# Loads queued further ahead in places shared with the weights, and output stores held back behind gating copies, in a fused attention and softplus kernel

## The chip, the cores and the metric

The kernel runs on one core of a Trainium2 chip. The metric is the device time of one execution in microseconds (us), the median of several runs. One execution per kernel is also profiled; its *span* is from first to last instruction. A run more than 1.5% above the fastest of its kernel counts as slow, and ratios use fast runs alone.

Engines: PE is TensorE (matmul), DVE VectorE, ACT ScalarE, POOL GpSimd, SP SyncE. DMA is the core's 16 DMA engines.

## The reference

Linear attention per head (8 batches, 8 heads, 576 positions, 64 features), then a two-layer network with a softplus.

```python
r = maximum(x, 0); phi(x) = concat([r * cos, r * sin])     # cos, sin of the position
kv  = einsum('bhsf,bhsd->bhfd', phi(k), v);  z = sum(phi(k), over s)
num = einsum('bhsf,bhfd->bhsd', phi(q), kv); den = einsum('bhsf,bhf->bhs', phi(q), z) + 1e-6
x   = (num / den), heads side by side                       # 4608 x 512
h   = x @ w_in                                              # 512 -> 2048
out = (maximum(h, 0) + log1p(exp(-abs(h)))) @ w_out         # 2048 -> 512
```

The softplus is replaced by its linear part where a bound on the norms of x and w_in allows it: `x @ (0.5 * w_in @ w_out) + ln 2 * sum(w_out)`. The kernel computes the bound while it runs, and a flag at the end chooses whether a slow exact branch must follow. With these inputs it need not.

## The kernel before

q, k and v are 3 x 8 loads of 1.18 MB in float32, converted to bf16 on the way and issued from GpSimd. The weights (8.4 MB) are loaded between batch 0 and batch 1. The output is made in 36 tiles of 128 tokens; a tile is 0.262 MB. The loads and the places they go to:

```python
loads = tile_pool(name="loads", bufs=3)                   # 3 places for each of q, k, v
kqv[b, name] = loads.tile([128, 4, T, D], BF16, tag=name)
w_out_sb = singles.tile([128, FO, D_MODEL], BF16)         # own places for the weights
w_inT    = singles.tile([128, FO, D_MODEL], BF16)
...
fetch(2)                                                  # right after batch 1's loads
```

One iteration of the main loop, for tile i (cut):

```python
attend(i)                       # PE: num, den; DVE: rden = 1/den, x = num * rden
scale_values(...)               # DVE: v * cos, v * sin of a later batch
if b + 3 < B and j == 1: fetch(b + 3)       # GpSimd: three loads
if ...: pool_relu(b + 2)        # GpSimd: rectify k, then q, of batch b + 2
if more and left < 2: key_values(b + 1, 1 - left)
turn_queries(i + 2)             # PE: q transposed and scaled; ACT: to SBUF
turn_x(i - 1)                   # PE: x transposed; ACT: to SBUF
finish(*emit(i - 2))            # PE: x @ W_c; DVE: + bias; then the store
```

The end of an iteration:

```python
def finish(n, ps):
    o_sb = outs.tile([128, D_MODEL], F32, tag="o_sb")     # 4 places
    nc.vector.tensor_add(o_sb, ps, b_bc)
    store(n, o_sb)                                        # SyncE: one DMA; two for a pair tile
```

Transposed queries of a whole batch share one tile (`qTs[b]`, three places of 9.2 KB per partition).

Of the kernel before, what the change touches and what calls it, by code (L numbers as in the profile page):

```python
# [21 lines left out]
def kernel(  # L22
# [25 lines left out]
    singles = ctx.enter_context(tc.tile_pool(name="singles", bufs=1))  # L48
    loads = ctx.enter_context(tc.tile_pool(name="loads", bufs=3))
    work = ctx.enter_context(tc.tile_pool(name="work", bufs=2))  # L50
# [17 lines left out]
    def load(b, name, part=None):  # L68
        if not part:
            kqv[b, name] = loads.tile([128, 4, T, D], BF16, tag=name, name=f"{name}_sb")  # L70
        hps = slice(0, 4) if part is None else slice(2 * part, 2 * part + 2)
        src = SRC[name][b].rearrange("(hp h2) (p t) d -> (h2 p) hp (t d)", h2=2, t=T)
        nc.gpsimd.dma_start(  # L73
            kqv[b, name].rearrange("p h t d -> p h (t d)")[:, hps], src[:, hps]
        )
# [10 lines left out]
    )  # L86
    w_out_sb = singles.tile([128, FO, D_MODEL], BF16)
    BLOCKS = 8
    FB = FO // BLOCKS
    w_in_r = moe_w_in.rearrange("(ko p) f -> p ko f", p=128)  # L90
    w_out_r = moe_w_out.rearrange("(fo p) m -> p fo m", p=128)

    warm = singles.tile([128, 2 * D_MODEL], BF16)
    nc.vector.memset(warm, 1.0)  # L94
# [11 lines left out]
    for j in range(BLOCKS):  # L106
        cols = slice(128 * FB * j, 128 * FB * (j + 1))
        nc.gpsimd.dma_start(w_in_sb[:, :, cols], w_in_r[:, :, cols])
        nc.gpsimd.dma_start(w_out_sb[:, FB * j : FB * (j + 1), :], w_out_r[:, FB * j : FB * (j + 1), :])

    w_sum = loads.tile([128, 2, D_MODEL], F32, tag="k", name="w_sum")
    w_tmp = loads.tile([128, 2, D_MODEL], F32, tag="v", name="w_tmp")
    load(1, "v")
# [58 lines left out]
    b_bc = singles.tile([128, D_MODEL], F32)  # L172
    w_inT = singles.tile([128, FO, D_MODEL], BF16)

# [18 lines left out]
    def turn_w_in(j):  # L193
        ps = o_ps.tile([128, FB, KO, 128], BF16, tag="o", name="wT_ps")
        for f in range(FB):
            for ko in range(KO):
                ft = FB * j + f
                nc.tensor.matmul(
                    ps[:, f, ko, :], w_in_sb[:, ko, ft * 128 : (ft + 1) * 128], ident,
                    is_transpose=True, start=True, stop=True, skip_group_check=True,  # L200
                )

        for f in range(FB):
            (nc.scalar.copy if f % 2 else nc.vector.tensor_copy)(
                view(w_inT, [256, 2], [64, 2], [128, 2], [1, 64], offset=(FB * j + f) * D_MODEL),
                view(ps, [256, 2], [128, 2], [64, 2], [1, 64], offset=f * D_MODEL),
            )
# [3 lines left out]
    def square_w(ft):  # L211
        if ft % 2 or ft >= 10:
            nc.scalar.activation(
                w_square[:, 0, :], w_inT[:, ft, :], ACT.Square, bias=zero_b,
                accum_out=w_norm[:, ft : ft + 1],
            )
        else:
            nc.vector.scalar_tensor_tensor(
                w_square[:, 1, :], w_inT[:, ft, :], 1.0, w_inT[:, ft, :], ALU.mult, ALU.mult,
                accum_out=w_norm[:, ft : ft + 1],  # L220
            )

    def fold(j, ps):
        order = [(ft, g) for ft in range(FB * j, FB * (j + 1)) for g in range(KO)]
        if j == BLOCKS - 1:
            order.sort(key=lambda x: x[1])
        for ft, g in order:
            nc.tensor.matmul(  # L228
                ps[g // 2][:, g % 2, :], w_inT[:, ft, g * 128 : (g + 1) * 128], w_out_sb[:, ft, :],
                start=(ft == 0), stop=(ft == FO - 1),  # L230
            )


    def sum_w_out(quarter):
        rows = w_out_sb[:, 4 * quarter : 4 * quarter + 4, :]
        nc.vector.tensor_add(w_tmp if quarter else w_sum, rows[:, :2, :], rows[:, 2:, :])
        if quarter:
            nc.vector.tensor_add(w_sum, w_sum, w_tmp)
            nc.vector.tensor_add(w_tmp[:, 0, :], w_sum[:, 0, :], w_sum[:, 1, :])

    def bias():
        ps = o_ps.tile([128, D_MODEL], F32, tag="o", name="b_ps")
        nc.tensor.matmul(ps, ones, w_tmp[:, 0, :], start=True, stop=False)
        for ft in range(8, FO):
            nc.tensor.matmul(ps, ones_b, w_out_sb[:, ft, :], start=False, stop=(ft == FO - 1))
        nc.scalar.mul(b_bc, ps, LN2)
# [60 lines left out]
    def turn_queries(n, pool=None, split=False):  # L307
        ps = (pool or qt_ps).tile([128, 2, 512], F32, tag="big" if pool else "qt", name="q_ps")
        if len(tiles[n]) == 1:
            b, t = tiles[n][0][0], tiles[n][0][1] // 64  # L310
            if b not in qTs:
                qTs[b] = work.tile([128, 2, 4, S], BF16, tag="qT", name="qT", bufs=3)
            parts = [(b, hq, t + t2) for hq in range(2) for t2 in range(2)]
            moves = [(view(qTs[b], [4 * S, 2], [64, 2], [S, 4], [1, 64], offset=64 * t), ps)]
        else:
            parts = [(p[0], hq, T - 1) for p in tiles[n] for hq in range(2)]
            moves = [
                (view(qTs[p[0]], [4 * S, 2], [S, 4], [1, 64], offset=512), ps[:, j])
                for j, p in enumerate(tiles[n])
            ]  # L320
        for j, (b, hq, t) in enumerate(parts):
# [3 lines left out]
                start=True, stop=True, skip_group_check=True,  # L325
            )
        if split:
            moves = [
                (view(qTs[b], [64, 2], [S, 4], [1, 64], offset=64 * (t - 1) + hq * 4 * S), ps[:, hq])
                for hq in range(2)  # L330
            ]
        for j, (dst, src) in enumerate(moves):
            copy = nc.vector.tensor_copy if split and j else nc.scalar.copy
            copy(dst, view(src, [1, 1024 // len(moves)]))  # L334

    xs = {}

    def attend(n, pool=None):
# [7 lines left out]
        for g in range(4):  # L346
            hq, h2 = g // 2, g % 2
            for b, t0, m, p0 in tiles[n]:
                for c in range(2):
                    for i in range(2):  # L350
                        rows = slice(64 * i, 64 * i + 64)
                        nc.tensor.matmul(  # L352
                            num[p0 : p0 + m, i, C * g : C * g + C],
                            qTs[b][rows, hq, 2 * c + h2, t0 : t0 + m],
                            blk_bufs[b % 3][rows, hq, h2, c, :], start=False, stop=(c == 1),
                            skip_group_check=True,
                        )
        rden = small.tile([128, 2, 4], F32, tag="rden")
        nc.vector.reciprocal(rden, view(num, [512, 2], [C, 4], offset=D))
        if n % 2 == 0:  # L360
            xs[n // 2] = outs.tile([128, 2, 4, 2, D], BF16, tag="x", name="x", bufs=4)
# [36 lines left out]
    def emit(n, ps=None):  # L398
# [4 lines left out]
        return n, ps  # L403

    def finish(n, ps):
        o_sb = outs.tile([128, D_MODEL], F32, tag="o_sb")
        nc.vector.tensor_add(o_sb, ps, b_bc)  # L407
        store(n, o_sb)

# [32 lines left out]
    for j in range(BLOCKS + 1):  # L442
# [22 lines left out]
        if j == 6:  # L465
            mark_values(1)
    for hq in range(2):
        for c in range(2):
# [16 lines left out]
    turn_queries(5, big_ps)  # L485
    fetch(3)
    pool_relu(2)
    LEAD = 2

# [4 lines left out]
    for b in range(1, B):  # L494
# [6 lines left out]
        for j, i in enumerate(mine):  # L501
# [5 lines left out]
            if j == len(mine) - 1 and b + 2 < B:  # L507
                scale_values(b + 2, *SCALES[0])
            if b + 3 < B and j == 1:
                fetch(b + 3)  # L510
            if b + 2 < B and j == (3 if b == 1 else 2):
                pool_relu(b + 2)
            left = mine[-1] - i
            if more and left < 2:
# [29 lines left out]
    with tc.If(flag < 1):  # L544
        one_b = small.tile([128, 1], F32, tag="one_b", bufs=1)
        nc.vector.memset(one_b, 1.0)
        w_g = [view(vcs_bufs[g // 2], [1, D_FF], offset=g % 2 * D_FF) for g in range(KO)]
        for ft in range(FO):
            ps = qt_ps.tile([128, KO, 128], BF16, tag="qt", name="w_ps")
            for g in range(KO):  # L550
                nc.tensor.matmul(
                    ps[:, g, :], w_inT[:, ft, g * 128 : (g + 1) * 128], ident,
                    is_transpose=True, start=True, stop=True, skip_group_check=True,
                )
            for g in range(KO):
                nc.vector.tensor_copy(w_g[g][:, ft * 128 : (ft + 1) * 128], ps[:, g, :])
        for n in range(len(tiles)):
            soft = loads.tile([128, FO, 128], BF16, tag="k", name="soft")
            for quarter in range(4):
                h = qt_ps.tile([128, 4, 128], F32, tag="qt", name="h_ps")  # L560
                for j in range(4):
                    ft = 4 * quarter + j
                    for g in range(KO):
# [3 lines left out]
                        )  # L567
                e = outs.tile([128, 4, 128], F32, tag="o_sb", name="e")
                nc.scalar.activation(e, h, ACT.Abs, bias=zero_b)
# [6 lines left out]
            for ft in range(FO):  # L576
                nc.tensor.matmul(
                    ps, soft[:, ft, :], w_out_sb[:, ft, :], start=(ft == 0), stop=(ft == FO - 1)
                )
            o_sb = outs.tile([128, D_MODEL], F32, tag="o_sb")  # L580
            nc.vector.tensor_copy(o_sb, ps)
# [31 lines left out]
```

## Time and profile before

| | before |
|---|---|
| time, median of 3 | 142.99 us (142.59 to 143.39) |
| profiled run | 145.22 us, span 143.3 (slow: over 1.5% above the fastest) |
| busy: PE, DVE, ACT, POOL | 118.8, 105.4, 94.7, 66.4 us |
| read from HBM, written | 36.70 MB, 9.44 MB |
| chain that ended last | 63% of the span is waiting for DMA |

The chain that ended last, by engine (shares of the span):

```profile
DMA 63%; POOL 10%; issue 10%; PE 7%; ACT 5%; DVE 0%; POOLq 0%
```

The chain starts at the last instruction and steps back to whatever released it each time. That nearly two thirds of it are DMA says that the end moves when loads move; it doesn't say whether they are late because they were issued late or because the engines were busy with something else. The lines in the prediction are about that.

### The profile page before, as it was taken

Reading aid. Unit: us, or ns where it says so; the run is one execution under the profiler, and the core shown is the slowest. Engines: PE = TensorE matmul, PEld = TensorE weight load, DVE = VectorE, ACT = ScalarE, POOL = GpSimd, SP = SyncE. Lnnn points to the kernel's source line nnn. Section 1 sums busy time; section 2 is a strip of 40 time slices with the busy share of each in tenths; the row PEclk is TensorE's granted clock in tenths of the full one; section 3 lists DMA queues with packets and bytes.
Section 4 is the critical chain, followed back from the end, with each engine's and each line's share of the span. In section 5 each row is a group of like instructions: output and inputs, shape, how many; then the busy total and the mean of one; then the engine's idle time right before and its main releaser. Section 6 shows DMA issues by size and latency. Waiting matters only on the chain.

```text
span 143.3 us, 4481 instructions
## 1 busy us (share of the span) xinstructions
PE 118.8 (83%) x1890; PEld 76.1 (53%) x1890; DVE 105.4 (74%) x219; ACT 94.7 (66%) x165; POOL 66.4 (46%) x83
## 2 busy tenths in 40 slices
PE   4927978999799999997899979799889729998810
PEld 1414455666345657774666746476666516665300
DVE  2499244797798589989889988779969953576920
ACT  3401194597698476898599978599969904998500
POOL 7995455564018089266856825936620570000000
PEclk9996599999999999999999999999999986999975
DMA  1999999999999999999999999999999730233350
GB/s 12 176 186 198 205 197 201 200 201 206 207 206 209 209 236 271 242 255 249 240 245 260 254 254 251 249 250 238 260 246 258 219 77 0 90 134 146 136 170 11
DMA packets 24410, 28.14 MB, mean 196 GB/s; under 512 B 1344, under 2 KB 19776, under 8 KB 24384
## 3 DMA queue, kind: packets, MB, share of 16 engines
q0 software_dynamic: 19136, 18.35, 78.2%
q1 hardware_dynamic: 5248, 9.44, 19.7%
q8 instruction: 17, 0.28, 0.7%
q14 instruction: 9, 0.07, 0.1%
HBM read 36.70 MB, written 9.44 MB: 322 GB/s over the span
## 4 chain that ended last, share of the span: by engine, by line
DMA 63%; POOL 10%; issue 10%; PE 7%; ACT 5%; DVE 0%; POOLq 0%
DMA q_sb<-in_q_dram 43%; DMA w_out_sb<-in_moe_w_out_dram 15%; DMA v_sb<-in_v_dram 5%; POOL q_r L258 4%; POOL k_sb L73 3%; PE o_ps L402 3%; ACT qT L334 2%; POOL v_sb L73 2%; ACT x L380 2%; PE q_ps L322 1%; PE o_big L402 1%; ACT xT_all L375 1%; PE xT_ps L371 1%; PE num_ps L352 1%; POOL q_sb L73 1%
## 5 line engine op out<-in xcount | busy, mean ns | idle before, releaser
L334 ACT CAST qT<-q_ps 128x1024 bf16<-128x1024 f32 (+1 forms) x40 | 35.7, 909 | 17.8 <-PE q_ps L322 17.8
L402 PE MATMUL o_ps<-W_c,xT_all 128*128 128x512 bf16 x132 | 34.8, 387 | 0.7 <-DVE o_sb L407 0.6
L407 DVE TENSOR_TENSOR o_sb<-o_ps,b_bc 128x512 f32<-128x512 f32 x33 | 22.6, 686 | 13.4 <-PE o_ps L402 13.4
L275 DVE TENSOR_TENSOR vcs<-v_sb,cs_wide 128x1152 bf16<-128x1152 bf16 x32 | 29.7, 944 | 0.0
L322 PE MATMUL q_ps<-diag,q_r 128*128 128x256 bf16 x144 | 23.3, 283 | 7.7 <-POOL q_r L258 5.9
L362 DVE TENSOR_TENSOR x<-num_ps,rden 128x512 bf16<-128x512 f32 x36 | 24.9, 692 | 2.1
L251 POOL TENSOR_SCALAR k_sb<-k_sb 128x1152 bf16<-128x1152 bf16 x12 | 14.7, 1232 | 22.8 <-DMA k_sb<-in_k_dram 22.8
L258 POOL TENSOR_SCALAR q_r<-q_sb 128x1152 bf16<-128x1152 bf16 x13 | 16.8, 1312 | 15.8 <-DMA q_sb<-in_q_dram 15.8
L375 ACT CAST xT_all<-xT_ps 128x512 bf16<-128x512 f32 x36 | 21.5, 598 | 1.2 <-PE xT_ps L371 1.2
L380 ACT ACTIVATE x<-x,zero_b 128x1024 bf16<-128x1024 bf16 x17 | 19.8, 1162 | 0.0
L322 PEld LDWEIGHTS <-q_r 128*128 128x128 bf16 x144 | 12.1, 100 | 13.5 <-POOL q_r L258 7.3
L402 PEld LDWEIGHTS <-xT_all 128*128 128x128 bf16 x144 | 12.9, 99 | 10.3 <-issue 1.6
L352 PE MATMUL num_ps<-kvblk,qT 64*128 64x65 bf16 (+1 forms) x640 | 15.8, 194 | 0.0
L228 PE MATMUL wc_ps<-w_out_sb,w_inT 128*128 128x512 bf16 x64 | 15.0, 380 | 0.0
L289 PE MATMUL kv_ps<-vcs,k_sb 64*64 64x132 bf16 x576 | 11.8, 225 | 3.7 <-DVE vcs L275 3.7
L294 ACT CAST kvblk<-kv_ps 128x260 bf16<-128x260 f32 x16 | 6.0, 376 | 11.5 <-PE kv_ps L289 11.0
L371 PE MATMUL xT_ps<-perm,x 128*128 128x128 bf16 x128 | 12.7, 222 | 0.6 <-ACT xT_all L375 0.6
L289 PEld LDWEIGHTS <-k_sb 64*64 64x64 bf16 x576 | 9.5, 110 | 5.8 <-issue 4.4
L371 PEld LDWEIGHTS <-x 128*128 128x128 bf16 x144 | 10.8, 99 | 2.2 <-issue 0.6
L352 PEld LDWEIGHTS <-qT 64*128 64x128 bf16 (+1 forms) x640 | 11.4, 98 | 0.8
L342 PEld LDWEIGHTS <-warm 128*128 128x128 bf16 x72 | 6.9, 99 | 9.1 <-issue 2.1
L414 PE MATMUL spin_ps<-warm 128*128 128x512 bf16 x28 | 9.4, 498 | 2.0 <-DVE warm L94 2.0
(75 smaller groups left out, 131.8 us busy)
## 6 DMA issues: line engine op xcount, KB each, us to landing
out_dram<-o_sb SPq DMA_DIRECT2D x32, 256.0 KB, 6.2
v_sb<-in_v_dram POOLq DMA_DIRECT2D x7, 576.0 KB, 14.5
k_sb<-in_k_dram POOLq DMA_DIRECT2D x7, 576.0 KB, 16.9
q_sb<-in_q_dram POOLq DMA_DIRECT2D x6, 576.0 KB, 20.3
xT_all<-in_moe_w_in_dram POOLq DMA_DIRECT2D x8, 256.0 KB, 10.5
w_out_sb<-in_moe_w_out_dram POOLq DMA_DIRECT2D x8, 256.0 KB, 10.6
q_sb<-in_q_dram POOLq DMA_DIRECT2D x4, 288.0 KB, 10.5
out_dram<-o_sb SPq DMA_DIRECT2D x8, 128.0 KB, 3.9
```

What stands on the lines that cost most here:

```text
L258: engine.tensor_scalar(q_rs[b][:, hq], view(kqv[b, "q"], [D, T], [T * D, 2], [1, D], offset=2 * hq * T * D), BIG, 0.0, ALU.min, ALU.max,)
L275: nc.vector.tensor_mul(view(vcs, [T * 2 * VW, 2], [2 * VW, T], [1, D], offset=2 * hq * T * 2 * VW + c * VW), kqv[b, "v"][:, 2 * hq : 2 * h ...
L289: nc.tensor.matmul(kv[64 * i : 64 * i + 64, h2, :, :VW], k_r[rows, 2 * hq + i, t, :], vcs[rows, 2 * hq + i, t, :, :], start=(t == 0), stop ...
L322: nc.tensor.matmul(ps[:, j // 2, 256 * (j % 2) : 256 * (j % 2) + 256], q_rs[b][:, hq, t, :, :], diag[:, t, :, :], start=True, stop=True, s ...
L334: copy(dst, view(src, [1, 1024 // len(moves)]))
L352: nc.tensor.matmul(num[p0 : p0 + m, i, C * g : C * g + C], qTs[b][rows, hq, 2 * c + h2, t0 : t0 + m], blk_bufs[b % 3][rows, hq, h2, c, :], ...
L362: nc.vector.tensor_mul(xs[n // 2][:, n % 2], view(num, [C, 4], [512, 2], [1, D]), view(rden, [1, 4], [4, 2], [0, D]),)
L371: nc.tensor.matmul(ps[:, g, :], x[:, g, :, :], perm if len(tiles[n]) == 1 else ident, start=True, stop=True, skip_group_check=True,)
L375: nc.scalar.copy(xT_all[:, n], ps)
L380: nc.scalar.activation(x, x, ACT.Square, bias=zero_b, accum_out=x_norm[:, n : n + 1])
L402: nc.tensor.matmul(ps, xT_all[:, n, g, :], W_c[:, g, :], start=(g == 0), stop=(g == 3))
L407: nc.vector.tensor_add(o_sb, ps, b_bc)
```

## The change

The intent: stores and loads run on the same DMA engines, and the loads are urgent while the stores are not. So up to 11 finished tiles are held in SBUF, and their stores go out when the loads are nearly done. Moreover loads get more places, which the weights use first (their tiles die early), and batch 3 is fetched before GpSimd first stops to rectify. SBUF for the held tiles comes from transposed queries kept by tile rather than by batch.

```diff
-    loads = ctx.enter_context(tc.tile_pool(name="loads", bufs=3))
+    loads = ctx.enter_context(tc.tile_pool(name="loads", bufs=6))
+            kqv[b, name] = loads.tile(... tag=name, bufs=4 if name == "q" else 6)
-    w_out_sb = singles.tile([128, FO, D_MODEL], BF16)
-    w_inT = singles.tile([128, FO, D_MODEL], BF16)
+        if j % 2 == 0:
+            w_out_tiles.append(loads.tile([128, 4, D_MODEL], BF16, tag="k", ...))
+            w_inT_tiles.append(loads.tile([128, 4, D_MODEL], BF16, tag="v", ...))
... (w_sum and w_tmp move to the places of q; fetch(3) moves up, fetch(b + 3) becomes fetch(b + 4))
-                qTs[b] = work.tile([128, 2, 4, S], BF16, tag="qT", name="qT", bufs=3)
+        qT = qTs[n] = work.tile([128, 2, 4, 128], BF16, tag="qT", name="qT", bufs=4)
...
         nc.vector.reciprocal(rden, view(num, [512, 2], [C, 4], offset=D))
+        pass_stores(n, rden)
...
+    HOLD = 11
+    held = []
+    passed = singles.tile([1, 4, 8], F32)
+    def pass_stores(i, rden):
+        keep = HOLD - 1 - 3 * max(0, i - 27)
+        if len(held) > keep:
+            nc.sync.dma_start(passed[:, i % 4, :], rden[:1].rearrange("p i g -> p (i g)"))
+        while len(held) > max(0, keep):
+            store(*held.pop(0))
     def finish(n, ps):
-        o_sb = outs.tile([128, D_MODEL], F32, tag="o_sb")
+        o_sb = outs.tile([128, D_MODEL], F32, tag="o_sb", bufs=HOLD + 3)
         nc.vector.tensor_add(o_sb, ps, b_bc)
-        store(n, o_sb)
+        held.append((n, o_sb))
+        if n > last - 3:
+            while held:
+                store(*held.pop(0))
... (the exact branch, not taken here, loads its weights again)
```

The gating copy is a DMA of 32 bytes that copies a tile's reciprocals to nowhere in particular. The stores stand behind it in SyncE's program, so while SyncE waits for the reciprocal of tile i, they wait too: in the changed kernel the first store goes out at 72.98 us, right after the first copy, and without the copies at 48.01 (e7 below).

More of the change, by code (lines that the diff above doesn't have):

```diff
@@ L69, in load @@
         if not part:
-            kqv[b, name] = loads.tile([128, 4, T, D], BF16, tag=name, name=f"{name}_sb")
+            kqv[b, name] = loads.tile(
+                [128, 4, T, D], BF16, tag=name, name=f"{name}_sb", bufs=4 if name == "q" else 6
+            )
         hps = slice(0, 4) if part is None else slice(2 * part, 2 * part + 2)
@@ L86, with w_out_rows, w_inT_rows @@
     )
-    w_out_sb = singles.tile([128, FO, D_MODEL], BF16)
     BLOCKS = 8
     FB = FO // BLOCKS
+    w_out_tiles, w_inT_tiles = [], []
+    def w_out_rows(ft, count=1):
+        return w_out_tiles[ft // 4][:, ft % 4 : ft % 4 + count, :]
+    def w_inT_rows(ft):
+        return w_inT_tiles[ft // 4][:, ft % 4, :]
     w_in_r = moe_w_in.rearrange("(ko p) f -> p ko f", p=128)
     w_out_r = moe_w_out.rearrange("(fo p) m -> p fo m", p=128)
-    warm = singles.tile([128, 2 * D_MODEL], BF16)
+    warm = singles.tile([128, D_MODEL], BF16)
     nc.vector.memset(warm, 1.0)
@@ L108 @@
         nc.gpsimd.dma_start(w_in_sb[:, :, cols], w_in_r[:, :, cols])
-        nc.gpsimd.dma_start(w_out_sb[:, FB * j : FB * (j + 1), :], w_out_r[:, FB * j : FB * (j + 1), :])
-    w_sum = loads.tile([128, 2, D_MODEL], F32, tag="k", name="w_sum")
-    w_tmp = loads.tile([128, 2, D_MODEL], F32, tag="v", name="w_tmp")
+        if j % 2 == 0:
+            w_out_tiles.append(loads.tile([128, 4, D_MODEL], BF16, tag="k", name="w_out_sb"))
+            w_inT_tiles.append(loads.tile([128, 4, D_MODEL], BF16, tag="v", name="w_inT"))
+        nc.gpsimd.dma_start(w_out_rows(FB * j, FB), w_out_r[:, FB * j : FB * (j + 1), :])
+    w_sum = loads.tile([128, 2, D_MODEL], F32, tag="q", name="w_sum", bufs=4)
+    w_tmp = loads.tile([128, 2, D_MODEL], F32, tag="q", name="w_tmp", bufs=4)
     load(1, "v")
@@ L204, in turn_w_in @@
             (nc.scalar.copy if f % 2 else nc.vector.tensor_copy)(
-                view(w_inT, [256, 2], [64, 2], [128, 2], [1, 64], offset=(FB * j + f) * D_MODEL),
+                view(w_inT_rows(FB * j + f), [256, 2], [64, 2], [128, 2], [1, 64]),
                 view(ps, [256, 2], [128, 2], [64, 2], [1, 64], offset=f * D_MODEL),
@@ L213, in square_w @@
             nc.scalar.activation(
-                w_square[:, 0, :], w_inT[:, ft, :], ACT.Square, bias=zero_b,
+                w_square[:, 0, :], w_inT_rows(ft), ACT.Square, bias=zero_b,
                 accum_out=w_norm[:, ft : ft + 1],
@@ L218, in square_w @@
             nc.vector.scalar_tensor_tensor(
-                w_square[:, 1, :], w_inT[:, ft, :], 1.0, w_inT[:, ft, :], ALU.mult, ALU.mult,
+                w_square[:, 1, :], w_inT_rows(ft), 1.0, w_inT_rows(ft), ALU.mult, ALU.mult,
                 accum_out=w_norm[:, ft : ft + 1],
@@ L228, in fold @@
             nc.tensor.matmul(
-                ps[g // 2][:, g % 2, :], w_inT[:, ft, g * 128 : (g + 1) * 128], w_out_sb[:, ft, :],
+                ps[g // 2][:, g % 2, :], w_inT_rows(ft)[:, g * 128 : (g + 1) * 128], w_out_rows(ft)[:, 0],
                 start=(ft == 0), stop=(ft == FO - 1),
@@ L234, in sum_w_out @@
     def sum_w_out(quarter):
-        rows = w_out_sb[:, 4 * quarter : 4 * quarter + 4, :]
+        rows = w_out_rows(4 * quarter, 4)
         nc.vector.tensor_add(w_tmp if quarter else w_sum, rows[:, :2, :], rows[:, 2:, :])
@@ L244, in bias @@
         for ft in range(8, FO):
-            nc.tensor.matmul(ps, ones_b, w_out_sb[:, ft, :], start=False, stop=(ft == FO - 1))
+            nc.tensor.matmul(ps, ones_b, w_out_rows(ft)[:, 0], start=False, stop=(ft == FO - 1))
         nc.scalar.mul(b_bc, ps, LN2)
@@ L308, in turn_queries @@
         ps = (pool or qt_ps).tile([128, 2, 512], F32, tag="big" if pool else "qt", name="q_ps")
+        qT = qTs[n] = work.tile([128, 2, 4, 128], BF16, tag="qT", name="qT", bufs=4)
         if len(tiles[n]) == 1:
             b, t = tiles[n][0][0], tiles[n][0][1] // 64
-            if b not in qTs:
-                qTs[b] = work.tile([128, 2, 4, S], BF16, tag="qT", name="qT", bufs=3)
             parts = [(b, hq, t + t2) for hq in range(2) for t2 in range(2)]
-            moves = [(view(qTs[b], [4 * S, 2], [64, 2], [S, 4], [1, 64], offset=64 * t), ps)]
         else:
-            parts = [(p[0], hq, T - 1) for p in tiles[n] for hq in range(2)]
-            moves = [
-                (view(qTs[p[0]], [4 * S, 2], [S, 4], [1, 64], offset=512), ps[:, j])
-                for j, p in enumerate(tiles[n])
-            ]
+            parts = [(p[0], hq, T - 1) for hq in range(2) for p in tiles[n]]
         for j, (b, hq, t) in enumerate(parts):
@@ L327, in turn_queries @@
         if split:
-            moves = [
-                (view(qTs[b], [64, 2], [S, 4], [1, 64], offset=64 * (t - 1) + hq * 4 * S), ps[:, hq])
-                for hq in range(2)
-            ]
-        for j, (dst, src) in enumerate(moves):
-            copy = nc.vector.tensor_copy if split and j else nc.scalar.copy
-            copy(dst, view(src, [1, 1024 // len(moves)]))
+            for hq in range(2):
+                (nc.vector.tensor_copy if hq else nc.scalar.copy)(
+                    view(qT, [64, 2], [128, 4], [1, 64], offset=512 * hq), ps[:, hq]
+                )
+        else:
+            nc.scalar.copy(view(qT, [512, 2], [64, 2], [128, 4], [1, 64]), view(ps, [1, 1024]))
     xs = {}
@@ L353, in attend @@
                             num[p0 : p0 + m, i, C * g : C * g + C],
-                            qTs[b][rows, hq, 2 * c + h2, t0 : t0 + m],
+                            qTs[n][rows, hq, 2 * c + h2, p0 : p0 + m],
                             blk_bufs[b % 3][rows, hq, h2, c, :], start=False, stop=(c == 1),
@@ L357, in attend @@
                         )
-        rden = small.tile([128, 2, 4], F32, tag="rden")
+        rden = small.tile([128, 2, 4], F32, tag="rden", bufs=6)
         nc.vector.reciprocal(rden, view(num, [512, 2], [C, 4], offset=D))
+        pass_stores(n, rden)
         if n % 2 == 0:
@@ L466 @@
             mark_values(1)
+            fetch(3)
     for hq in range(2):
@@ L485 @@
     turn_queries(5, big_ps)
-    fetch(3)
     pool_relu(2)
+    fetch(4)
     LEAD = 2
@@ L508 @@
                 scale_values(b + 2, *SCALES[0])
-            if b + 3 < B and j == 1:
-                fetch(b + 3)
             if b + 2 < B and j == (3 if b == 1 else 2):
                 pool_relu(b + 2)
+                if b + 4 < B:
+                    fetch(b + 4)
             left = mine[-1] - i
@@ L547 @@
         w_g = [view(vcs_bufs[g // 2], [1, D_FF], offset=g % 2 * D_FF) for g in range(KO)]
-        for ft in range(FO):
-            ps = qt_ps.tile([128, KO, 128], BF16, tag="qt", name="w_ps")
-            for g in range(KO):
-                nc.tensor.matmul(
-                    ps[:, g, :], w_inT[:, ft, g * 128 : (g + 1) * 128], ident,
-                    is_transpose=True, start=True, stop=True, skip_group_check=True,
-                )
-            for g in range(KO):
-                nc.vector.tensor_copy(w_g[g][:, ft * 128 : (ft + 1) * 128], ps[:, g, :])
+        for g in range(KO):
+            for i in range(2):
+                rows = (4 * (g // 2) + 2 * i + g % 2) * D
+                nc.gpsimd.dma_start(w_g[g][64 * i : 64 * i + 64], moe_w_in[rows : rows + D, :])
+        w_out_tiles.clear()
+        for j in range(4):
+            w_out_tiles.append(loads.tile([128, 4, D_MODEL], BF16, tag="k", name="w_out_sb"))
+            nc.gpsimd.dma_start(w_out_rows(4 * j, 4), w_out_r[:, 4 * j : 4 * j + 4, :])
         for n in range(len(tiles)):
-            soft = loads.tile([128, FO, 128], BF16, tag="k", name="soft")
+            soft = loads.tile([128, FO, 128], BF16, tag="v", name="soft")
             for quarter in range(4):
@@ L567 @@
                         )
-                e = outs.tile([128, 4, 128], F32, tag="o_sb", name="e")
+                e = outs.tile([128, 4, 128], F32, tag="o_sb", name="e", bufs=HOLD + 3)
                 nc.scalar.activation(e, h, ACT.Abs, bias=zero_b)
@@ L577 @@
                 nc.tensor.matmul(
-                    ps, soft[:, ft, :], w_out_sb[:, ft, :], start=(ft == 0), stop=(ft == FO - 1)
+                    ps, soft[:, ft, :], w_out_rows(ft)[:, 0], start=(ft == 0), stop=(ft == FO - 1)
                 )
-            o_sb = outs.tile([128, D_MODEL], F32, tag="o_sb")
+            o_sb = outs.tile([128, D_MODEL], F32, tag="o_sb", bufs=HOLD + 3)
             nc.vector.tensor_copy(o_sb, ps)
```

## The prediction

> **What bounds the kernel now.** I read the page's slices first. Slices are 3.58 us wide, and the three rows that matter here are the matmul engine, the DMA engines and the bytes moved:
>
> ```profile
> PE   4927978999799999997899979799889729998810
> DMA  1999999999999999999999999999999730233350
> GB/s 12 176 186 198 205 197 201 200 201 206 207 206 209 209 236 271 242 255 249 240 245 260 254 254 251 249 250 238 260 246 258 219 77 0 90 134 146 136 170 11
> ```
>
> The DMA engines are never idle until slice 31 (111 us), then they are two thirds empty to the end. PE is also near full, except for one hole in slice 32 (115 to 118 us). Next, what the bytes are: the loads convert float32 to bf16 on the way, so a load reads twice the bytes it lands, and the queue view says who moved what.
>
> ```profile
> q0 software_dynamic: 19136, 18.35, 78.2%
> q1 hardware_dynamic: 5248, 9.44, 19.7%
> HBM read 36.70 MB, written 9.44 MB: 322 GB/s over the span
> ```
>
> Queue q0 holds the loads, q1 the stores. Before any store (20 to 30 us) the windows view gives 200 GB/s landed, so 400 GB/s read. In 75 to 85 us it gives 253 GB/s; about four stores of 0.262 MB are 105 of it, the loads then land 148 and read 296: again 401 GB/s of memory traffic. So loads and stores share one budget of about **0.40 MB/us**, and a store delays the loads by 0.262/0.40 = 0.66 us.
>
> The chain of waits that ended last says where that hurts (start, us, what):
>
> ```profile
> 93.30 21.47 DMA q_sb<-in_q_dram
> ...
> 114.92 2.77 POOL q_r L258 x2
> 117.69 0.05 issue
> 117.73 0.61 PE q_ps L322 x2
> ```
>
> The last batch's queries land at 114.77 us; GpSimd rectifies them, and only then can PE turn them. From there 25.6 us of compute and stores follow to 143.3. How regular is the rest? VectorE makes one reciprocal per tile of 128 tokens (36 tiles), so its timeline is a clock of progress (start, us):
>
> ```profile
> 49.89 0.20 DVE L359 RECIPROCAL rden<-num_ps 128x8 f32<-128x8 f32 x1
> 70.75 0.20 DVE L359 RECIPROCAL rden<-num_ps 128x8 f32<-128x8 f32 x1
> 82.39 0.20 DVE L359 RECIPROCAL rden<-num_ps 128x8 f32<-128x8 f32 x1
> 114.20 0.19 DVE L359 RECIPROCAL rden<-num_ps 128x8 f32<-128x8 f32 x1
> 121.12 0.20 DVE L359 RECIPROCAL rden<-num_ps 128x8 f32<-128x8 f32 x1
> ```
>
> These are tiles 4, 12, 17, 29 and 30. Tiles 12 to 17 take 2.33 us each; 4 to 12 take 2.61; 17 to 29 take 2.65; tile 29 to 30 alone takes 6.92. So there is a compute pace near 2.35 and, on top, waits for loads: small ones in each batch and one of about 4 us at the end. The waits of 105 to 120 us agree:
>
> ```profile
> POOL k_sb L251 <- DMA k_sb<-in_k_dram: 6.0, 1, 6.0
> PE q_ps L322 <- POOL q_r L258: 3.3, 2, 2.1
> DVE o_sb L407 <- PE o_ps L402: 1.5, 2, 1.1
> ```
>
> So the start is DMA bound (to 42.4 us, when batch 1's queries are in), then compute and DMA are nearly matched, with DMA slightly slower.
>
> **What the Trainium skill says.** "DMA: Bandwidth & Descriptors", section "Queues, rings and completion order": each DMA engine goes round-robin between its queue rows packet by packet, so stores from SyncE and loads from GpSimd slow each other. The trace agrees (0.40 MB/us with or without stores). "HBM Reference", section "Access": one core streaming alone reaches about 425 GB/s; this trace has 400 to 416. "DMA: Bandwidth & Descriptors", section "Anatomy of one DMA": some 2 us of fixed cost per DMA, mostly completion; no gating copy runs in the kernel before, but its smallest landing time, 2.3 us for a store in the quiet tail, fits. "SBUF — State Buffer", section "Who interferes with whom": a VectorE instruction with two SBUF inputs and a GpSimd one that reads SBUF block each other. In the trace the value scaling takes 0.75 us, and up to 1.73 where GpSimd rectifies; the change leaves those, so I count them in the pace.
>
> **The change part by part.**
>
> (1) Deeper load buffers, the weights in shared places, batch 3 fetched before batch 2 is rectified. This keeps two batches queued, where one and a bit was. By itself I give it **0 us**: the DMA row is at 9 throughout to 111 us, so no load was issued too late for the engines to stay busy. The order of instructions on GpSimd shows that the new early loads wait for buffers freed by the folding of the weights and for the DMA eight issues back, all done before 42.4 us, so the start doesn't get longer.
>
> (2) Stores held. Up to 11 finished tiles wait; tile n is stored after the reciprocal of tile n+13 rather than after its own bias add, which comes during iteration n+2. At most 11 x 0.262 = 2.88 MB is out of the loads' way, worth 2.88/0.40 = 7.2 us of load time. When do loads end then? At 42.4 us batches 2 to 7 remain: 6 x 3 x 1.18 = 21.2 MB. At pace 2.38 (my estimate between 2.33 and 2.42, the pace of tiles 4 to 9, 49.89 to 62.00 us), the first store comes with tile 13, at 49.9 + 9 x 2.38 = 71.3 us. Till then 28.9 x 0.40 = 11.6 MB are read; the remaining 9.7 MB share with stores of 0.262/2.38 = 0.11 MB/us, so take 9.7/0.29 = 33.4 us: **loads end near 104.7 us** in place of 114.8. At 0.385 MB/us, the slowest stretches of this trace, it is 108.
>
> (3) Is that soon enough? With no wait, tile 29's reciprocal stands at 49.9 + 25 x 2.38 = 109.4 us. The last queries are wanted there, rectified, so they should land by some 3 us earlier, 106.4. With 104.7 there is no hole; with 108 one of about 2 us. Tile 30 follows 2.75 us after tile 29 (an iteration with keys times values): 112.1 in place of 121.1, **a gain of 9.0 us**, and the tail from there is unchanged (22.2 us): 134.3.
>
> (4) Gating copies: 23 DMAs of 32 bytes in SyncE's queue. They cost no engine time; SyncE spends about 0.54 us per issue, as for a store. 23 + 40 issues x 0.54 = 34 us over 70 us: it keeps up.
>
> (5) Queries turned into a tile of their own rather than a batch's: the split copies of the four pair tiles (two of 0.53 us) become one of 1.01: 0. The smaller warm-up tile: under 0.3 us in a start that loads bound: 0.
>
> (6) A new wait. An output buffer is used again after 14 tiles, and the store of tile n-14 is issued only after the reciprocal of n-1. From there to the bias add of tile n are three iterations and 1.5 us, 8.6 us; a gating issue, a store issue and a landing of 6.2 (5.9 to 7.6 under load) take 7.3 to 8.7 us. Just covered; I charge 0.3 us. Bursts of four stores at tiles 28, 29 and 30 drain at 4 x 0.66 = 2.6 us per iteration, about one iteration each, while 30 us remain; if the last load is still coming they delay it.
>
> Sum: 143.0 - 9.0 + 0.3 = 134.3; for half a chance of a remaining hole of about 2 us I add 1.1: **135.4 us**.
>
> **The rivals.**
>
> (a) Compute is already the bound, and only the hole goes: PE, VectorE and ScalarE are each over 90% busy in 75 to 85 us. Then the pace stays 2.6 and only 6.92 - 2.75 = 4.2 us are won: 138.8. For it: the full engines. Against: every batch has a wait of PE for rectified queries, and tiles 12 to 17 ran at 2.33.
>
> (b) The new wait takes its place: VectorE waits for stores to land before each bias add from tile 14 on. If a landing takes 8 us with the gate and not 6, each loop of three tiles is 1 to 2 us longer, some 5 us in all over the 15 held tiles: 139 to 140. For it: the margin of (6) is thin. Against: landings over 7 us are rare in this trace.
>
> (c) The bursts at 28 and 29 meet the last load. Eight stores are 5.2 us of traffic; if loads run late these come on top: q at 110, end at 138. It needs loads at 108 or later.
>
> (d) The held stores become the tail. 21 tiles after tile 27 are 5.5 MB, 13.8 us at 0.40 MB/us, with 30 us left: unlikely; +1 at most.
>
> **Range and chances.** Between no hole with a pace of 2.33 (133) and rival (b) or (c) (139.5): 132.5 to 139.5. Over 2% faster means below 140.1, which even the rivals mostly give: 0.89. Within 2%: 0.09, if two of the rivals come together. Slower: 0.02.
>
> **What the changed profile would show.** GB/s near 205 until about 70 us, then 250: no stores before tile 13. The last q landing at 104 to 108 us, and in the reciprocals a step from tile 29 to 30 below 4 us. The pace from tile 4 to 29 near 2.4. VectorE's bias adds waiting for DMA under 1 us in all. A DMA row that is higher after 110 us than the present 2 to 3 tenths. I am wrong if the loads end before 106 us and the pace is still 2.6 (rival a), if the bias adds wait for stores (b), or if GB/s doesn't stay at the 0.40 budget when the stores go.

## The result, and the profile after

| | before | after |
|---|---|---|
| time, median of 4 | 143.06 us (142.59 to 143.39) | 137.16 us (136.77 to 137.93) |
| ratio of fast runs | | 0.9596, 95% interval 0.9546 to 0.9647 |
| span of the profiled run | 143.3 (slow run) | 136.1 (fast run) |
| spans of all four runs | | 136.1, 134.9, 135.5, 135.1 |

A ratio is the mean time of one kernel's fast runs over that of the other's of the same rounds, so it isn't quite the ratio of the medians. A span is 1.8 to 1.9 us shorter than the time of that same run (136.1 against 137.93, 143.3 against 145.22). The change is 4.0% faster; the predicted 135.4 us (132.5 to 139.5) was 1.8 us too low, and the range holds the result.

The slices of the changed kernel's page (now 3.40 us each):

```profile
PE   5926959999699998998969998999999999989400
DMA  1999999999999999999999999999996365776480
GB/s 8 179 184 200 201 202 199 200 202 202 207 207 207 208 207 210 207 209 207 208 209 207 228 262 256 253 251 256 241 277 208 117 205 200 288 245 234 180 289 15
```

GB/s now stays at 200 to 210 until slice 21 (71 to 75 us): nothing but loads. Then it rises to some 250, loads and stores. The DMA row falls at slice 30 (102 us) and afterwards stands mostly at 5 to 8 tenths in place of 2 to 3: the held stores. PE has no hole like the one at 115 us any more.

The chain that ended last, by engine:

```profile
PE 49%; DVE 22%; ACT 15%; issue 6%; POOL 2%; ACTq 0%; POOLq 0%; DVEq 0%
```

DMA has left the chain altogether. GpSimd's timeline (start, us of two instructions, and in brackets the idle time and what ended it) shows the last queries landing just before 105.62:

```profile
105.62 2.76 POOL L269 TENSOR_SCALAR q_r<-q_sb 128x1152 bf16<-128x1152 bf16 x2 [2.06 <-DMA q_sb<-in_q_dram]
```

VectorE's reciprocals, tiles 4, 29, 30 and 35:

```profile
47.96 0.20 DVE L364 RECIPROCAL rden<-num_ps 128x8 f32<-128x8 f32 x1
110.07 0.20 DVE L364 RECIPROCAL rden<-num_ps 128x8 f32<-128x8 f32 x1
112.53 0.20 DVE L364 RECIPROCAL rden<-num_ps 128x8 f32<-128x8 f32 x1
123.81 0.20 DVE L364 RECIPROCAL rden<-num_ps 128x8 f32<-128x8 f32 x1
```

From 29 to 30 it is now 2.46 us, not 6.92. But from tile 35 to the end of the span it is 12.3 us, where the kernel before took 10.8 (132.50 to 143.3). SyncE's own timeline explains why (start, us for the group, and how many):

```profile
119.16 1.25 SPq L402 DMA_DIRECT2D out_dram<-o_sb  x2
120.51 0.68 SPq L420 DMA_DIRECT2D passed<-rden  x1
121.23 1.22 SPq L400 DMA_DIRECT2D out_dram<-o_sb  x2
...
126.74 0.69 SPq L420 DMA_DIRECT2D passed<-rden  x1
127.84 1.85 SPq L400 DMA_DIRECT2D out_dram<-o_sb  x3
129.79 1.21 SPq L402 DMA_DIRECT2D out_dram<-o_sb  x2
```

The gating copy at 126.74 belongs to tile 35, whose reciprocal had been ready since 124.0: SyncE is nearly 3 us behind. From 108.12 to 131.0 it issues 8 copies and 24 stores, 32 issues in 22.9 us, almost without pause. The span ends 5.1 us after SyncE's last issue, and in e5 below, whose last issue comes earlier, 5.2 us after it.

### The profile page after: what moved, and what is told of

It reads as the page before. It is cut to its first block, busy times and chain, and to the rows that moved or that the text cites. A ratio compares the mean times of both kernels' runs of the same rounds, so it can differ in the third digit from the quotient of the medians.

```text
span 136.1 us, 4522 instructions
## 1 busy us (share of the span) xinstructions
PE 114.9 (84%) x1890; PEld 74.7 (55%) x1890; DVE 102.6 (75%) x219; ACT 94.5 (69%) x161; POOL 66.5 (49%) x83
## 4 chain that ended last, share of the span: by engine, by line
PE 49%; DVE 22%; ACT 15%; issue 6%; POOL 2%; ACTq 0%; POOLq 0%; DVEq 0%
PE o_ps L408 11%; PE q_ps L327 9%; DVE vcs L286 8%; ACT qT L339 8%; PE wc_ps L239 8%; PE kv_ps L300 6%; PE num_ps L357 5%; PE xT_ps L377 3%; DVE o_sb L426 3%; DVE x L368 3%; ACT xT_all L381 3%; ACT x L386 3%; DVE diag L161 2%; PE wT_ps L209 2%; PE o_big L408 1%
## 5 line engine op out<-in xcount | busy, mean ns | idle before, releaser
L339 ACT CAST qT<-q_ps 128x1024 bf16<-128x1024 f32 x34 | 34.3, 1014 | 8.2 <-PE q_ps L327 8.1
L408 PE MATMUL o_ps<-W_c,xT_all 128*128 128x512 bf16 x132 | 33.9, 379 | 0.8 <-DVE o_sb L426 0.7
L286 DVE TENSOR_TENSOR vcs<-v_sb,cs_wide 128x1152 bf16<-128x1152 bf16 x32 | 28.0, 891 | 0.6 <-DMA v_sb<-in_v_dram 0.6
L327 PE MATMUL q_ps<-diag,q_r 128*128 128x256 bf16 x144 | 21.9, 274 | 1.6 <-issue 0.5
L377 PE MATMUL xT_ps<-perm,x 128*128 128x128 bf16 x128 | 12.4, 219 | 0.6 <-ACT xT_all L381 0.6
L436 PE MATMUL spin_ps<-warm 128*128 128x512 bf16 x28 | 8.6, 468 | 1.5 <-DVE warm L104 1.5
```

The lines of the kernel that those rows point to most:

```text
L286: nc.vector.tensor_mul(view(vcs, [T * 2 * VW, 2], [2 * VW, T], [1, D], offset=2 * hq * T * 2 * VW + c * VW), kqv[b, "v"][:, 2 * hq : 2 * h ...
L327: nc.tensor.matmul(ps[:, j // 2, 256 * (j % 2) : 256 * (j % 2) + 256], q_rs[b][:, hq, t, :, :], diag[:, t, :, :], start=True, stop=True, s ...
L339: nc.scalar.copy(view(qT, [512, 2], [64, 2], [128, 4], [1, 64]), view(ps, [1, 1024]))
L377: nc.tensor.matmul(ps[:, g, :], x[:, g, :, :], perm if len(tiles[n]) == 1 else ident, start=True, stop=True, skip_group_check=True,)
L408: nc.tensor.matmul(ps, xT_all[:, n, g, :], W_c[:, g, :], start=(g == 0), stop=(g == 3))
```

## The experiments

e0 and e10 are the kernel before, e4 is the changed kernel and e5 is e3 again. All the others were timed beside the kernel before on the same chip. Medians are of all runs. For reading them together, these are positions in each profile (us of the span): when GpSimd starts to rectify the last queries, the reciprocal of tile 30, and the tail from tile 35's reciprocal to the end.

| run | stores held | last q rectified | tile 30 | tail | time, median | ratio (95%) |
|---|---|---|---|---|---|---|
| before, first profile (slow run) | 0 | 114.92 | 121.12 | 10.8 | 142.99 | |
| e0 before | 0 | 113.87 | 118.81 | 11.0 | 142.94 | |
| e10 before | 0 | 114.55 | 119.08 | 10.8 | 142.95 | |
| e1 deep loads alone (slow run) | 0 | 114.38 | 119.81 | 11.1 | 143.10 | 1.003 (0.996 to 1.009) |
| e7 no gates | 0 in effect | 113.98 | 118.50 | 10.9 | 142.26 | 1.000 (0.992 to 1.007) |
| e6 five held | 5 | 111.75 | 116.19 | 10.8 | 140.84 | 0.987 (0.976 to 0.999) |
| changed | 11 | 105.62 | 112.53 | 12.3 | 137.16 | 0.960 (0.955 to 0.965) |
| e4 changed (slow run) | 11 | 106.31 | 113.07 | 12.3 | 137.84 | 0.960 (0.954 to 0.966) |
| e2 hold alone | 11 | 106.17 | 112.17 | 12.4 | 137.52 | 0.959 (0.949 to 0.968) |
| e3 tail ungated | 11 | 106.02 | 112.77 | 10.9 | 136.75 | 0.961 (0.954 to 0.967) |
| e5 tail ungated | 11 | 105.81 | 111.31 | 10.5 | 136.40 | 0.958 (0.953 to 0.963) |
| e8 first 15 stores left out | all | 99.47 | 113.53 | 12.1 | 137.79 | 0.963 (0.958 to 0.968) |
| e11 little rectifying | 11 | | 110.97 | 11.9 | 135.68 | 0.951 (0.945 to 0.957) |

**e0 and e10: the kernel before, profiled again.** No edit.

> The kernel before, unchanged, for a second profile: the first one fell in an execution 2.2 us longer than the median. I expect a span near 141.1 us (143.0 less the 1.9 us by which the first profile's time exceeds its span). Theory A (the lost 2 us belong to the wait for the last queries): the step from tile 29 to 30 is about 2 us shorter than 6.92, all else alike. Rival: the extra time is spread over the start, and the step stays near 6.9.

> The kernel before once more, for a third profile of it: span about 141. Theory F (chance): its start has no cold stretch, or tile 4's reciprocal stands near 48 us; theory G: cold again somewhere in 10 to 28 us, tile 4 at 49.5 us or later.

Both have a span of 141.1 us, as expected for a fast run. Their reciprocals of tile 30, e0's and then e10's:

```profile
118.81 0.20 DVE L359 RECIPROCAL rden<-num_ps 128x8 f32<-128x8 f32 x1
119.08 0.20 DVE L359 RECIPROCAL rden<-num_ps 128x8 f32<-128x8 f32 x1
```

In e0 the step from tile 29 to 30 is 2.66 us, and a long one of 6.06 stands between tiles 20 and 21 instead; in e10 it is 3.78. The step shrank by 4.3 us and not by 2, with other waits elsewhere, so neither theory A nor its rival holds as it was put. The hole at 115 us wasn't a fixed feature of the end: the loads bind all along, and where the wait shows varies. What doesn't vary is when the last queries come (113.9 to 114.9). Tile 30 stands at 119 in these fast runs, not at 121.1: 2 us of the difference that the prediction subtracted belonged to a slow run.

The other question was the granted clock of TensorE in the start. TensorE's work is nearly the same up to about 42 us in all these kernels, yet the first held profiles had no cold stretch there (slices in which the granted clock falls well below full speed) and the first unheld ones did (tenths of full speed in 40 slices; e0, then e10):

```profile
PEclk9999995999999999999999999968999999999995
PEclk9999999999999999999999999999999999999995
```

e10 is the kernel before without a cold stretch, tile 4 at 47.93 us rather than 49.53. Later e8, a held kernel, had one (tile 4 at 49.71). So theory G falls: the stretch comes by chance in kernels of both kinds, and what sets it off stays open. And it costs the kernel before nothing: e0 and e10 reach tile 12 at 70.41 and 70.36, since the loads bind by then.

**e1: the deeper loads alone.** The changed kernel with its stores issued at once:

```diff
-        pass_stores(n, rden)
-        held.append((n, o_sb))        # and the rest of the hold
+        store(n, o_sb)
```

> The changed kernel with its deeper loads and shared places, but every store issued at once after its bias add, as before (no gating copy, 4 output buffers). Theory A (only the held stores move the loads): 143 us, within 0.7 of the kernel before; last q landing at 112 to 115 us of the span; a hole at tile 29 to 30. Rival B (the loads were issued too late, and the depth of the queue gives the gain): 137 to 138 us and a last q near 106 us.

1.003 (0.996 to 1.009): nothing. GpSimd's timeline (the profile fell in a slow run) still has the last queries at 114 us:

```profile
114.38 2.25 POOL L269 TENSOR_SCALAR q_r<-q_sb 128x1152 bf16<-128x1152 bf16 x2 [0.82 <-DMA q_sb<-in_q_dram]
```

Rival B falls. The DMA engines had never lacked a queued load (their row stands at 9 until 111 us in the kernel before), so a longer queue in front of them had nothing to gain.

**e2: the hold alone.** The changed kernel with the loads of before: three places each, own places for the weights, `fetch` where it was:

```diff
-    loads = ctx.enter_context(tc.tile_pool(name="loads", bufs=6))
+    loads = ctx.enter_context(tc.tile_pool(name="loads", bufs=3))
+    w_out_sb = singles.tile([128, FO, D_MODEL], BF16)
+    w_inT = singles.tile([128, FO, D_MODEL], BF16)
... (fetch(3) after turn_queries(5), fetch(b + 3) at j == 1)
```

> The changed kernel with the loads, buffers and places for weights of the kernel before (three buffers each), but its stores held by gating copies. Theory A: 137.2 us like the changed kernel, within 0.7; last q at 104 to 107 us. Rival B: 142 to 143 us, because loads come too late without the depth. Rival C (both parts needed): in between, 139 to 141, with DMA below 9 tenths in some slices before 100 us.

0.959 (0.949 to 0.968), 137.52 us: all of the gain. The last queries come when they do in the changed kernel:

```profile
106.17 2.73 POOL L265 TENSOR_SCALAR q_r<-q_sb 128x1152 bf16<-128x1152 bf16 x2 [2.10 <-DMA q_sb<-in_q_dram]
```

A version of this that kept the old query tiles as well didn't build: the output pool wanted 36 KB per partition and 17.9 were left. So the part of the change that the hold needs is the smaller query tile, not the sharing of places with the weights.

**e7: the hold without its gates.** Same order of stores in SyncE's program, no copies:

```diff
-        if len(held) > keep:
-            nc.sync.dma_start(passed[:, i % 4, :], rden[:1].rearrange("p i g -> p (i g)"))
```

> The changed kernel with the gating copies taken out; the stores stand as late in SyncE's program as in the changed kernel. Theory H (only the copy's wait for a later reciprocal holds a store; SyncE otherwise runs ahead to it as soon as its tile is ready): first store at about 46 us, 143 us, like e1_deep_only. Rival (place in the program is enough): first store near 72 us, 137 us.

1.000, with the first store out at 48.01 us (SyncE's timeline), not 72.98:

```profile
48.01 17.32 SPq L400 DMA_DIRECT2D out_dram<-o_sb  x8
```

Place in the program held nothing here: SyncE has no other work, so it runs ahead to the next store and issues it as soon as its tile is ready. Only a wait for something later held it.

**e6: five held tiles.**

```diff
-    HOLD = 11
+    HOLD = 5
```

> The changed kernel with 5 held tiles in place of 11 (8 output buffers in place of 14). Theory A with the traffic budget of 0.40 MB/us: five tiles move the loads by 5 x 0.66 = 3.3 us; the end then lies at 143.0 - 3.3 = 139.7 us if loads still bind, last q at 109 to 111 us. Rival (compute is the bound and a few held tiles already free it): 137.5 us, like 11. Rival (nothing below a threshold): 142 or more.

The last queries are rectified from 111.75 us, and the ratio is 0.987 (0.976 to 0.999), so some 1.8 us are won, where the budget of 0.66 us per tile promised 3.3. The start of the last rectifying moved by 2.4 us from the mean of 114.2 of the unheld profiles e0, e10, e1 and e7, 0.5 us per tile; with 11 tiles (changed and e4) it moved by 7.9 to 8.6, 0.7 to 0.8 per tile. The direction is right and the size isn't. In this run SyncE's queue releases stores at 107.88 us and from 110.87 on, while the last queries are still coming, which works against the hold (rival c of the prediction); that this is the whole of the shortfall wasn't tested.

**e8: no store before tile 28.** The stores of tiles 0 to 14 are left out, so the result is wrong:

```diff
-            store(*held.pop(0))
+            done = held.pop(0)
+            if done[0] >= 15:
+                store(*done)
```

> The changed kernel with the stores of tiles 0 to 14 left out (wrong result on purpose: these rows stay unwritten), gating copies kept. No store shares the engines with loads before tile 28, so the loads end near 42.4 + 21.2/0.40 = 95.5 us. Theory C (11 held tiles already made compute the bound): reciprocals of tiles 29 and 30 at 110 and 112.5 us as before, time 136.5 to 137.2. Rival (loads still bind): tile 30 at 109 or earlier, time 133 to 135.

The loads end near 95 us, some 10 us earlier still, as the DMA row shows; it drops in slice 27 (92 to 96 us), near the expected 95.5:

```profile
DMA  1999999999999999999999999996000046876480
```

Yet the time is 137.79 us, ratio 0.963 (0.958 to 0.968), and tile 30 stands at 113.53. The last rectifying now waits for TensorE, which turns an earlier batch's queries, and not for its load:

```profile
99.47 2.76 POOL L269 TENSOR_SCALAR q_r<-q_sb 128x1152 bf16<-128x1152 bf16 x2 [3.38 <-PE q_ps L327]
```

So with 11 held tiles the loads no longer bind: taking 15 stores out of their way altogether gives nothing more in time. Theory C holds, though its 136.5 to 137.2 was 0.6 low. This profile began with a cold stretch; counted from tile 4 its pace is 2.45 us per tile, at the edge of the 2.45 to 2.52 of the five profiles that hold 11 (changed, e2 to e5), so a few tenths of a us left to the loads can't be excluded.

**e3 and e5: no gating copies in the tail.**

```diff
-        if len(held) > keep:
+        if len(held) > keep and i < 31:
```

> The changed kernel without the gating copies of tiles 31 to 35, where nothing is left to hold. Theory D (SyncE's issue rate bounds the tail: it issues back to back from 108 to 131 us): five issues of 0.67 us less, the last store issued some 2 us earlier, end limited by the flag after the last bias add: 135.6 to 136.2 us. Rival E (the DMA engines or the landing of the last stores bound the tail): 136.9 to 137.3, no change.

> The changed kernel, unchanged, beside the next three on one chip, with more rounds. 137.2 us, ratio 0.960. Its first stretch (reciprocals of tiles 0 to 4) took 27.2 us in its first profile against 28.8 to 28.9 in the three kernels that don't hold stores; theory F (chance of the granted clock in the start) expects profiles of held kernels to show a cold stretch in some runs, theory G (something in the changed start) never.

> The same kernel as e3_tail_ungated, with five rounds beside the changed kernel. Theory D: the profile of e3 gave a tail (from the last reciprocal to the end) of 10.85 us against 12.3, so its time is 0.8 to 1.4 us below that of e4_changed_again. Rival E: the tails differ, but what follows waits for something else, and the times agree within 0.4 us.

e4 is the changed kernel, on the same chip and in the same rounds as e5. The tails are clear: 10.9 and 10.5 us without the copies, 11.9 to 12.4 in every kernel that holds 11 and keeps them (changed, e2, e4, e8, e11), and 10.8 to 11.1 in every kernel that holds none. The copies alone don't do it: e6 keeps them to the end, with fewer held stores to release, and its tail is 10.8. In e5 SyncE is no longer behind; its last issue follows the last bias add:

```profile
117.77 1.25 SPq L402 DMA_DIRECT2D out_dram<-o_sb  x2
119.05 7.21 SPq L400 DMA_DIRECT2D out_dram<-o_sb  x8
126.76 1.15 SPq L402 DMA_DIRECT2D out_dram<-o_sb  x2
```

In time it shows less surely. The fast runs of e5 have a mean of 135.95 us (134.92, 136.69, 136.06, 136.11), those of e4 136.74 (136.9, 137.18, 136.15): 0.8 us, at the low end of what was expected, and the intervals of the two ratios overlap. e3, the same kernel as e5 on the same chip, has a mean of 136.83, no better than e4's, and at a median of 136.75 missed its 135.6 to 136.2; both together have a mean of 136.39, 0.4 us below e4's. So the tail is shown to be SyncE's in the traces, but what it is worth in time, 0.8 us or less, isn't settled; e5 is the fastest correct kernel by its median.

**e9 and e11: the interference of GpSimd.** In batches 2 to 7 GpSimd rectifies a ninth of the columns, and PE turns unrectified queries; wrong on purpose.

```diff
-            relu_k(b, nc.gpsimd, slice(2 * hq, 2 * hq + 2))      # and relu_q
+                # for name in ("k", "q"), for hq in range(2):
+                part = kqv[b, name][:, 2 * hq : 2 * hq + 2, 0, :]
+                nc.gpsimd.tensor_scalar(part, part, BIG, 0.0, ALU.min, ALU.max)
... (PE reads q_sb in place of q_r; the flag is changed)
```

> The changed kernel with GpSimd's rectifying of batches 2 to 7 cut to a ninth of the columns (wrong result on purpose; the query turns read unrectified queries in place, and the flag is loosened so that the other branch isn't taken). Theory P (GpSimd's reads hold up VectorE's value scaling, and that is why the pace is 2.48 us per tile and not 2.38): the scaling falls from 0.89 to 0.75 us in the mean, 28 x 0.14 = 3.9 us of VectorE; the pace from tile 4 to 29 falls to 2.33 to 2.40 and the time by 2 to 3 us, 134.2 to 135.2. Rival (TensorE sets the pace): scaling at 0.75, pace still 2.45 or more, time within 0.7 us of 137.2.

> e9_small_relu once more, with the flag computed from the weights alone, so that the other branch isn't taken (in e9 it was, which made its time useless; its trace up to there had the value scaling at 0.75 us and a pace of 2.42 us from tile 4 to 29, with tile 29 at 110.2 us). Wrong result on purpose. Rival of theory P (TensorE sets the pace): 136.4 to 137.2 us. Theory P: 134.2 to 135.2 us.

In e9 the garbage tripped the flag in spite of a loosened bound, and the exact branch was taken: 1225 us, no use as a time. e11 takes the flag from the weights alone. The value scaling on VectorE, in the groups of instructions of the changed kernel and of e11 (busy us, mean ns, idle before):

```profile
L286 DVE TENSOR_TENSOR vcs<-v_sb,cs_wide 128x1152 bf16<-128x1152 bf16 x32 | 28.0, 891 | 0.6 <-DMA v_sb<-in_v_dram 0.6
```

```profile
L287 DVE TENSOR_TENSOR vcs<-v_sb,cs_wide 128x1152 bf16<-128x1152 bf16 x32 | 23.6, 752 | 1.1 <-DMA v_sb<-in_v_dram 1.1
```

It falls from 891 to 752 ns, 4.4 us of VectorE in all. This agrees with "SBUF — State Buffer", section "Who interferes with whom", which the prediction cites. The time falls to 135.68 us (0.951 against 0.960): some 1.3 us, between the two theories. The pace from tile 4 to 29 is (108.30 - 47.79)/25 = 2.42 us, against 2.48 (2.45 to 2.52 in the five profiles that hold 11; e9's trace, up to its branch, gives 2.42 too). So GpSimd's rectifying costs some 0.06 us per tile, by the scaling and perhaps by what else the smaller work frees, which the edit doesn't tell apart; without it the pace still isn't 2.38. What is left is PE, in the windows view of the changed kernel (from 88 to 110 us: length, then PE, PE weight load, DVE, ACT and POOL busy):

```profile
88.00:110.00 22.00, 21.51 (x462) 15.61 (x463) 19.68 (x36) 19.92 (x33) 10.65 (x9) 1.00 0.89 214
```

PE is busy 98% of the stretch, DVE and ACT 90%. That PE sets the rest of the pace is read from this line, not tested by an edit.

## Why the prediction was right or wrong

- **Bound and budget: right.** Loads and stores share one budget. In the changed kernel, loads alone land 208 GB/s, 416 read; the last loads end where 0.40 MB/us puts them (predicted 104.7 us, measured about 105.6), and the first store stands at 72.98 us (predicted 71.3). ("HBM Reference" states its 425 GB/s for a core streaming alone in its section "Specifications (TRN2)".) e6 is the one place where a tile was worth less (0.5 us) than the budget's 0.66.
- **Deeper loads worth 0: right**, e1 and e2 show it from both sides. (Batch 3 was fetched before batch 2 is rectified in the kernel before too; what moved is that it comes before batch 1's queries are rectified.)
- **No hole left: right.** Tile 30 was predicted at 112.1 us and stands at 112.53. That is luck in part, for two errors cancel in it: tile 4 came at 47.96 us and not at 49.9, because the first profile had a cold clock in the start (chance, e10), and the pace was 2.48 us and not 2.38. The pace came from two short stretches of a profile whose waits moved from run to run; e8 and e11 show that what remains is compute.
- **Gating copies "cost no engine time … it keeps up": wrong, the term of the sum that failed.** The prediction spread 63 issues over 70 us. But the release puts 32 of them into 22.9 us (108.12 to 131.0), at 0.54 to 0.70 each. The tail from tile 30, taken as unchanged at 22.2 us, is 23.6, 1.4 us longer; without the last five copies (e3, e5) it is as short as before.
- **The new wait for output buffers: right to charge little.** No bias add waits for DMA in the changed profile; VectorE's waits before them are for PE, 7.3 us in all.
- **The base of the sum: mis-sized.** The prediction set the profile's span of 143.3 us equal to the median time of 143.0. That span belonged to a slow run of 145.22 us; fast runs of the kernel before have spans of 140.3 to 141.6. So the gain of 9.0 us was taken from a tile 30 at 121.12 that stands near 119 in fast runs: 6.4 us is what the hold gives there, less 1.4 in the tail, about 5: that is the difference of the profiled spans, 141.1 and 136.1. In time it is 5.9, since the profiled run of the changed kernel was the slowest of its four. The 1.4 us that the prediction added for a new wait and for a hole, neither of which came, happened to cover the longer tail, which is luck too. Read as a span, 135.4 was what the four runs have (134.9 to 136.1); as a time it lacks the 1.8 to 1.9 us between span and time. (Half a chance of 2 us is 1.0 and not the 1.1 added, which changes nothing.)
- **Rivals.** (a), compute as the bound, is where the kernel has arrived, at a pace of 2.48 and not the feared 2.6. (b), stores that hold up VectorE, didn't happen. (c) may be what weakened e6. (d), the tail of held stores, was called unlikely, "+1 at most", and is what happened, with 1.4 us, through SyncE's issues rather than the traffic.

## What to carry to other kernels

Where a DMA queue is full throughout, as here, more buffers bring nothing (e1); ask instead what other traffic can go later, and price it by one budget for loads and stores. Holding a store needs a wait on something later, since an idle queue runs ahead of its place in the program; stop adding such waits where nothing is held any more, because the issuing engine has a budget too. And before subtracting microseconds found in a profile, see whether that profile was a fast run and what lies between its span and the measured time.

## What the Trainium skill lacked or had wrong

- "DMA: Bandwidth & Descriptors", section "Issuing engines are not separate DMA queues", calls the time to initiate a DMA "usually small relative to the DMA itself" and gives no figure for SyncE. Here an issue on SyncE took 0.54 to 0.70 us in the stretch from 108 to 131 us, for 32 bytes as for 256 KB. That is as much as the 0.66 us that 256 KB cost of the traffic budget, though small beside the 6.2 us from issue to landing in the kernel before. 32 issues in 22.9 us made the tail 1.4 us longer.
- The same page doesn't say which side of a converting load counts. Here the sum of bytes read and stored stayed at 0.39 to 0.42 MB/us, with the float32 side of the loads counted (208 GB/s landed as bf16 alone; 250 with 0.11 MB/us of stores among them).
- "TensorE: Matmul & The Clock Gate", section "Part 1: The HAM clock gate", puts the ramp penalty below 1% of a typical kernel span. That figure is for the ramp at the start; here 6 of 14 profiles had a further cold stretch between 10 and 28 us, with nearly the same TensorE work there as in the other eight. It put tile 4's reciprocal at 49.5 to 50.1 us in place of 47.8 to 48.0. Where loads were the bound it was absorbed (spans of 141.1 us with and without it, e0 and e10); where compute was, it stayed (tile 29 at 110.20 us in e9, with it, and at 108.30 in e11, without: 1.9 us, 1.4% of e11's span).
